# Filter samples on the tensor engine: four channels under one weight load

## The chip, the cores and the metric

One core of a Trainium2 chip runs the whole program. Its engines work side by side and are tied together by semaphores only: TensorE (PE; its weight loads are listed apart as PEld), VectorE (DVE), ScalarE (ACT), GpSimd (POOL) and SyncE (SP), the last two mostly as queues that issue DMAs. The metric is the device time of one execution in microseconds, as the median of several runs.

## The reference, cut to what matters

```python
def _A_ref(u, A_re, A_im, B_re, B_im, C_re, C_im, log_dt, Dskip):      # u: 1 x 2048 x 512
    dt = jnp.exp(log_dt)[:, None]
    A = A_re + 1j * A_im                                               # 512 channels x 128 states
    ...
    P = jnp.exp(logdA[:, :, None] * l[None, None, :])                  # l = 0 .. 2047
    K = jnp.einsum("dn,dnl,dn->dl", Cc, P, dB).real                    # 512 filters of 2048 samples
    ...                                                                # FFT of 4096: y = K * u along l
    y = (lambda x, *d: x.transpose(*d))(y, 0, 2, 1) + u * Dskip[None, None, :]

h = x + _A_ref(_layernorm(x), ...)
return h + _B_ref(_layernorm(h), ...)                                  # _B_ref: layernorm, w1 512x1376, gelu, w2
```

A layer norm, one long filter per channel, a residual, two more norms and an MLP with a residual. The filter K of a channel is the real part of a sum over 128 states of c_n times exp(a_n l). The change is in how samples of K are made.

## The kernel before

The 2048 rows are dealt over 128 partitions, 16 rows each. The filtering runs in the frequency domain with matmuls as transforms: the normed input goes through a first transform (`aps`, written to `A_dram` and read back as `X`), a second (`xps`, matrix `M`), is multiplied by the filter's spectrum (`kfps`), transformed back (`zps`), written to `Zd` and read back as `ZT`, and enters the MLP. The channels are worked in two halves of 256 (`hh` = 0 and 1).

The spectrum isn't computed from all 2048 samples but from some of them. A sample position is split in two: l = 8k + offset with k = 0..31 (tile `Pt`) and twenty offsets (tile `Q`, list `OFFS`). For state n (the partition) and channel c, `Pt[n, k, 0..1, c]` holds exp(8 k a_n) as two real components and `Q[n, m, 0..1, c]` holds c_n exp(OFFS[m] a_n) in the same way; the sum over n of the product of both is a matmul of a channel with itself: 32 rows (k) by 20 columns (m), and its real part is a combination of the two components.

How the operands come about, for each half (the functions are printed below):

- `exps`: ACT writes the amplitudes exp(8 k Re) into `Pt[:, k, 1, :]` (32 instructions of 256 channels) and those of `Q` (20), which DVE multiplies by `amp`. `Pt` and `Q` are one tile each for both halves, so the second half's exponentials wait until the matmuls of the first have read them (`o_get` on `o_kgen`).
- `p_half`, `q_half`: the phases are made on PE as a matmul with the tables `RP` and `RQ` (`outer`, from `wp`, `wq` and a folded identity), ACT takes the sine (`sines`, tiles `s` and `sq` in the ring of buffers `w`, WB = 6), DVE multiplies sine and amplitude (`mul`). For `Pt` the phases are made for k = 16..31 only; the lower k = 15..0 take the same sines with the other sign. A half has eight such steps for `Pt` (32 channels each) and ten for `Q`.
- `kgen`: four blocks a half. A block has 16 x 2 x 4 matmuls: 16 channels, two components, and four groups of channels that sit side by side in the array, each 32 columns wide (`tile_position`). Each matmul has its own weight load, 32 columns taken at a stride of 512 elements from `Pt`, and 20 columns at the same stride from `Q`. The two components stay apart in PSUM; ACT copies one (`ku`) and DVE adds or subtracts the other (`samples`, with `half_sign`). The first samples go to `KD_near`, the far ones to `KD_far`, each as one DMA, and five DMAs bring them back as `kt`, the weights' partner in the spectrum matmuls (`kfps`).

All this is written as some 620 operations with dependencies (`S.op`), and a list `ORDER` written out by hand says in which order they are issued and, where an operation may run on one of two engines, on which: `step >> 2` is the number of the operation, `step & 3` the choice. Every engine executes its share in the order of the list. The costs that stand with the operations are not used at run time. Ahead of `kgen` in the list stand the norms of the input (`norm`, `aps` and its eviction `a`), the parameters (`params`: phases `psi`, amplitude `amp`, the transposes `lps`), the transform tables (`tables`: `M`, `Mn`, `R`, `Rn`; the last rows through `last_row` and `put_rows`), all on the same engines. Behind it come `x_stage`, `conv` and `head_rows`, then `mlp`, which is plain code.

Of the kernel before, what the change touches and what calls it, by code (L numbers as in the profile page):

```python
# [23 lines left out]
TINY = 1e-30  # L24
EPS = 1e-5
# [3 lines left out]
WB = 6  # L29
AT = {"root": 2, "m0": 3, "m1": 3, "bases": 3, "sin0": 3, "exp": (1, 4), "sin": (3, 5)}  # L30
ORDER = [
# [154 lines left out]
def prefix(nc0, S, K, cp, ct, c2):  # L186
# [7 lines left out]
    K.deal = c2.tile([P, 2, 2, 4, 8], bf16, name="deal")  # L194
    g.memset(K.deal[:], 0.0)
    g.affine_select(out=K.deal[:], in_=K.deal[:], pattern=[[-64, 2], [-8, 2], [-16, 4], [-1, 8]], compare_op=ALU.not_equal, fill=1.0, base=0, channel_multiplier=1)
    K.deal = K.deal[:].rearrange("p h s g i -> p (h s g i)")
# [30 lines left out]
    split = ((3, 15), (0, 7), (0, 1), (1, 1), (4, 1))  # L228
    bits = c2.tile([P, 5], i32, name="bits")
    for n, (sh, m) in enumerate(split):  # L230
        ts(nc, bits[:, n:n + 1], pi[:], sh, ALU.logical_shift_right, m, ALU.bitwise_and)
    pf = ct.tile([P, 5], f32, name="pf")
    nc.vector.tensor_copy(pf[:], bits[:])
    t1, q, odd, b1, top16 = (pf[:, n:n + 1] for n in range(5))
    K.half_sign = ct.tile([P, 1], f32, name="half_sign")
    ts(nc, K.half_sign[:], top16, -2.0, ALU.mult, 1.0, ALU.add)
# [33 lines left out]

def outer(nc, S, K, pp, c2):

    K.RP = pp.tile([P, 16, 2, 32], bf16, name="RP")
    K.RQ = pp.tile([P, 20, 2, 16], bf16, name="RQ")
    m = c2.tile([P, 64], bf16, name="m64")
    wp = c2.tile([P, 16, 2], bf16, name="wp")
    wq = c2.tile([P, 20, 2], bf16, name="wq")
    g = nc.gpsimd
    count(nc, wp[0:96], 4, [[8, 16], [0, 2]])
    for n, v in enumerate((63.75, 64.0)):  # L280
        g.memset(wp[96:128, :, n:n + 1], v)
        g.memset(wq[96:128, :, n:n + 1], v)
    g.memset(wq[64:112], 1.0)
    for p0, p1, pieces in ((32, 64, ((0, 0, [[0, 8]]), (8, 1, [[0, 4]]), (12, 2, [[1, 2], [0, 2]]), (16, 4, [[1, 4]]))),
                           (64, 80, ((0, 0, [[0, 8]]), (8, 1, [[0, 4]]), (12, 2, [[1, 2], [0, 2]]), (16, 4, [[1, 4]]))),
                           (0, 48, ((0, 1, [[1, 8]]), (8, 2, [[2, 4]]), (12, 4, [[0, 2], [4, 2]]), (16, 8, [[0, 4]])))):
        for at, base, pattern in pieces:
            cnt = 1
            for _, c in pattern:
                cnt *= c  # L290
            count(nc, wq[p0:p1, at:at + cnt], base, pattern + [[0, 2]])
    pl = S.at(10.2)

    def fold():
        tt(nc, m[:], K.ident[:, 0:64], K.ident[:, 64:128], ALU.add)
        tt(nc, m[:, 0:32], m[:, 0:32], m[:, 32:64], ALU.add)
        tt(nc, m[:, 32:48], m[:, 0:16], m[:, 16:32], ALU.add)

    def make_p():
        tt(nc, K.RP[:].rearrange("p i c d -> p (i c) d"), bc(wp[:].rearrange("p i c -> p (i c)").unsqueeze(2), [P, 32, 32]), bc(m[:, 0:32].unsqueeze(1), [P, 32, 32]), ALU.mult)  # L300
# [38 lines left out]
def tables(nc, S, K, cp, mp, cv, ct, c2, psp, dram):  # L339
# [64 lines left out]
    bf = ct.tile([P, 4, 2, 16], f32, name="bf")  # L404
# [14 lines left out]
    def last_row():  # L419
# [4 lines left out]
        nc.vector.tensor_copy(bs[:], bf[:])  # L424
# [3 lines left out]
    b = S.op("DVE", 1.5, last_row, [f])  # L428
# [39 lines left out]
def params(nc, S, K, cp, pp, sc, cv, psp, raws, ldt, dtb, grb):  # L468
    T, S2, Z = {}, S.op, {}

    def step():
        for h in range(2):
            d = slice(HW * h, HW * h + HW)
            nc.scalar.activation(dtb[:, d].rearrange("p (s g i) -> p g s i", s=2, g=4), ldt[:, d].rearrange("p (g s i) -> p g s i", s=2, g=4), ACT.Exp)

    o_dt = S2("ACT", 0.8, step, [S.at(4.2)], fun=0, bias=600)
    for pair, t0 in ((("are", "aim"), 4.5), (("cre", "cim"), 5.6), (("bre", "bim"), 6.6)):
        cell = {}
        for n, nm in enumerate(pair):
            def tr(cell=cell, nm=nm, n=n):  # L480
                if not n:
                    cell["p"] = psp.tile([P, 2, 512], f32, name=f"tps_{nm}", tag="p", bufs=PB)
                for k in range(4):
                    nc.tensor.matmul(cell["p"][:, n, k::4], lhsT=raws[nm][:, k, :], rhs=K.deal, start=True, stop=True)
# [9 lines left out]
    nc.gpsimd.memset(src_p[:, :, 3, :], 3.0)  # L494
    nc.gpsimd.memset(src_q[:, :, 7, :], 3.0)
# [12 lines left out]
    w = [sc.tile([P, 512], f32, name=f"w{n}", tag="w", bufs=WB) for n in range(6)]  # L508
    t, cre, cim = [x[:] for x in w[0:4]], w[4][:], w[5][:]
    pc = sc.tile([P, 512], f32, name="pc", tag="ko", bufs=2)  # L510
    S.group, last = "six", S.group
    K.o_six = [S.op("NONE", 0.0, lambda: None, acq="w") for _ in range(6)]
# [17 lines left out]
    o_pc = S2(D, 1.5, lambda: frac(pc[:], psi[:], 124.0), [o_psw], bias=B - 20)  # L530
# [84 lines left out]
    def top():  # L615
        for h in range(2):
            d = slice(HW * h, HW * h + HW)
            nc.scalar.copy(K.top[0:1, d].rearrange("p (g s i) -> p g s i", s=2, g=4), cell["k"][:, d].rearrange("p (s g i) -> p g s i", s=2, g=4))
# [802 lines left out]
```

## Time and profile before

| | us |
|---|---|
| median of 3 runs | 273.11 |
| lowest, highest | 272.82, 273.22 |
| the profiled execution | 272.82 |
| its span, first to last instruction | 271.0 |

The profile is of one execution. Its span is 1.8 us shorter than the time of that same run, which also counts what lies around the instructions. PE is busy 236.1 us of the span, DVE 204.9, ACT 173.1, POOL 35.6. A row of a list in order of time begins with the start and the length of a run of like instructions, then engine, line, operation, tile written <- tiles read, shape, count, and in square brackets how long the engine had been idle and what it had waited for; "issue" is time in which it waited for nothing that the profile shows. Lines are those of the kernel printed above; a helper's line (L76, L88, L139) stands for many uses, which the tile names tell apart. The granted clock is that of PE, 1.00 being full speed.

### The profile page before, as it was taken

How to read it: one execution, taken by the hardware profiler on the slowest of the kernel's cores; microseconds unless marked ns; L12 is line 12 of the kernel's file. 1: busy time of each engine (PE TensorE's matmuls, PEld its weight loads, DVE VectorE, ACT ScalarE, POOL GpSimd, SP SyncE). 2: the span in 40 equal slices, each digit the busy share in tenths (PEclk: the TensorE clock that was granted, in tenths of full speed). 3: DMA queues.
4: the chain of work that ended last, by engine and by line, in shares of the span. 5: the costliest groups of instructions: out<-in, count | busy, mean ns of one | idle time of the engine just before them, and what ended most of it. 6: DMA issues, size and time to landing. Idle time of an engine off the chain costs nothing.

```text
span 271.0 us, 6046 instructions
## 1 busy us (share of the span) xinstructions
PE 236.1 (87%) x2380; PEld 151.6 (56%) x2380; DVE 204.9 (76%) x426; ACT 173.1 (64%) x293; POOL 35.6 (13%) x96
## 2 busy tenths in 40 slices
PE   3898348768769977999999999978999999999995
PEld 3433012325558754779988888766954444444443
DVE  4899999999999999998195969968572772772022
ACT  2999999998958999992644473716822621631710
POOL 8803850000001100000551001000000000000000
PEclk9755555999956999999999999999999999999999
DMA  5804945676957300120178598769824014014101
GB/s 160 284 3 60 182 131 155 175 217 213 290 182 212 64 0 0 41 80 5 51 175 228 182 232 236 193 177 285 213 41 114 2 40 116 0 22 102 34 19 59
DMA packets 50568, 33.71 MB, mean 124 GB/s; under 512 B 22602, under 2 KB 49084, under 8 KB 50284
## 3 DMA queue, kind: packets, MB, share of 16 engines
q1 hardware_dynamic: 49036, 29.69, 40.5%
q0 software_dynamic: 1504, 3.64, 5.2%
q8 instruction: 18, 0.29, 0.5%
q14 instruction: 10, 0.08, 0.1%
HBM read 18.65 MB, written 11.26 MB: 110 GB/s over the span
## 4 chain that ended last, share of the span: by engine, by line
PE 47%; DVE 30%; DMA 8%; issue 7%; ACT 5%; SPq 2%; DVEq 0%; ACTq 0%
PE h1ps L1228 14%; PE o2ps L1241 13%; PE kps L752 6%; DVE X L88 4%; DMA Zd<-z 4%; DVE st L819 4%; PE kfps L921 3%; DVE w L76 2%; DVE Q L670 2%; DVE a L88 2%; DVE Pt L76 1%; ACT sq L139 1%; ACT s L139 1%; DVE u L832 1%; DMA ZT<-Zd 1%
## 5 line engine op out<-in xcount | busy, mean ns | idle before, releaser
L1231 ACT ACTIVATE hT<-h1ps,b_sb 128x512 bf16<-128x512 f32 (+3 forms) x55 | 31.9, 604 | 40.8 <-PE h1ps L1228 40.8
L1228 PE MATMUL h1ps<-y2T,wide 128*128 128x512 bf16 (+3 forms) x220 | 40.7, 336 | 0.6 <-ACT y2T L86 0.5
L921 PE MATMUL kfps<-kt,M 128*128 128x256 bf16 x320 | 39.1, 273 | 0.0
L1241 PE MATMUL o2ps<-w_sb,hT 128*128 128x512 bf16 (+3 forms) x187 | 38.7, 366 | 0.0
L921 PEld LDWEIGHTS <-M 128*128 128x128 bf16 x320 | 31.3, 98 | 6.1 <-issue 2.6
L76 DVE TENSOR_TENSOR ot<-o2ps,h 128x512 bf16<-128x512 f32 (+1 forms) x17 | 10.9, 657 | 30.0 <-PE o2ps L1241 17.7
L1228 PEld LDWEIGHTS <-wide 128*128 128x128 bf16 (+1 forms) x220 | 21.9, 100 | 17.2 <-issue 0.6
L1241 PEld LDWEIGHTS <-hT 128*128 128x128 bf16 (+1 forms) x187 | 18.3, 98 | 19.7
L658 ACT ACTIVATE Pt<-th 128x256 bf16<-128x256 f32 x64 | 20.7, 401 | 2.6 <-DVE th L76 2.5
L752 PE MATMUL kps<-Q,Pt 128*32 128x20 bf16 x1024 | 19.1, 221 | 3.5 <-issue 2.6
L837 PE MATMUL aps<-u,BD 128*128 128x512 bf16 x32 | 12.1, 468 | 10.9 <-ACT u L830 6.9
L752 PEld LDWEIGHTS <-Pt 128*32 128x32 bf16 x1024 | 18.4, 169 | 5.6 <-issue 4.9
L139 ACT ACTIVATE sq<-qv 128x1024 bf16<-128x1024 int16 x20 | 20.3, 1069 | 0.2 <-PE qv L723 0.2
L76 DVE TENSOR_TENSOR Pt<-s,Pt 128x1024 bf16<-128x1024 bf16 x32 | 20.2, 683 | 0.0
L86 ACT CAST z<-zps 128x1024 bf16<-128x1024 f32 (+1 forms) x13 | 12.1, 957 | 8.3 <-PE zps L951 5.9
L139 ACT ACTIVATE s<-pv 128x1024 bf16<-128x1024 int16 x16 | 16.1, 1056 | 0.3 <-DVE Q L76 0.3
L76 DVE TENSOR_TENSOR h<-y,X 128x512 f32<-128x512 f32 (+1 forms) x12 | 9.3, 774 | 8.1 <-PE y L1192 6.0
L86 ACT CAST kf<-kfps 128x1024 bf16<-128x1024 f32 (+1 forms) x8 | 7.7, 959 | 10.4 <-PE kfps L921 10.3
L837 PEld LDWEIGHTS <-BD 128*128 128x128 bf16 x32 | 2.8, 103 | 19.1 <-DVE BD L76 6.6
L689 PE MATMUL pv<-RP,PQ 128*128 128x512 bf16 x32 | 10.8, 437 | 3.0 <-ACT sq L139 0.7
L76 DVE TENSOR_TENSOR Q<-sq,Q 128x1024 bf16<-128x1024 bf16 x20 | 13.3, 681 | 0.0
L442 POOL DMA_DIRECT2D Dp<-Dd x24 | 11.9, 503 | 9.1 <-DMA Dd<-ds 8.0
(234 smaller groups left out, 466.3 us busy)
## 6 DMA issues: line engine op xcount, KB each, us to landing
A_dram<-a SPq DMA_DIRECT2D x16, 256.0 KB, 2.5
X<-A_dram SPq DMA_DIRECT2D x4, 1024.0 KB
Zd<-z SPq DMA_DIRECT2D x15, 256.0 KB, 3.6
ZT<-Zd SPq DMA_DIRECT2D x11, 256.0 KB, 4.0
x<-in_A_u_dram SPq DMA_DIRECT2D x4, 512.0 KB, 7.8
X<-in_A_u_dram SPq DMA_DIRECT2D x4, 512.0 KB, 4.6
out_dram<-ot SPq DMA_DIRECT2D x15, 128.0 KB, 1.7
ZT<-Zd POOLq DMA_DIRECT2D x5, 256.0 KB, 5.0
```

Source lines behind the costliest of these rows:

```text
L76: (nc.vector if e == "DVE" else nc.gpsimd).tensor_tensor(out, a, b, op)
L86: nc.scalar.copy(out, in_)
L88: nc.vector.tensor_copy(out, in_)
L139: nc.scalar.activation(out, v.bitcast(i16)[..., 0:2 * n:2], ACT.Sin, scale=S2PI / 65536)
L442: nc.gpsimd.dma_start(t[o::128 // cnt], bass.AP(row.tensor, row.offset + 1024 * kh, [[0, cnt], [1, 1024]]))
L658: nc.scalar.activation(K.Pt[:, k, 1, :], K.th[:, ds], ACT.Exp, scale=float(8 * k))
L752: nc.tensor.matmul(kps[32 * g:32 * g + 32, i // 8, at:at + 20], lhsT=Pt[:, :, u, c], rhs=Q[:, :, u, c], start=True, stop=True, tile_positi ...
L837: nc.tensor.matmul(ps[:, h, :], lhsT=K.BD[:, h].rearrange("p a b -> p (a b)"), rhs=cell["u"][:], start=True, stop=True)
L921: nc.tensor.matmul(ps[:, k, c, :], lhsT=K.M[:, t, k0 + k, c, :], rhs=kt[:, t, :], start=(c == 1 and t == 0), stop=(t == 4))
L1228: nc.tensor.matmul(pt[:fs, 0:n], lhsT=K.w1_sb[:, dc, fc * P:fc * P + fs], rhs=(y2T[tb][:, dc, js, :] if tb or js.start else K.y2T[:, dc]). ...
L1231: nc.scalar.activation(hT[tb % 2][:fs, fc, cols], pt[:fs, 0:n], ACT.Gelu_apprx_tanh, bias=K.b1_sb[:fs, fc:fc + 1], scale=1.0)
L1241: nc.tensor.matmul(pt[:], lhsT=h[:fs, fc, jj * P:(jj + 1) * P], rhs=K.w2_sb[:fs, fc, d], start=(fc == 0), stop=(fc == NFC - 1))
```

## The change

Four channels are now the columns of one weight load: `Pt` is laid out as component, group of four channels, k, channel, so that 32 k times 4 channels lie in one piece of 128. One matmul multiplies it with the 20 offsets of the same four channels, 80 columns. Of the 128 x 80 results the blocks where both channels are the same are used. Component 0 and 1 go into the same PSUM columns one after the other, so their sum is formed there; for that sum to be the real part the phases are turned by an eighth of a turn (`EIGHTH`, `TURN`).

```diff
+TURN = 9.0
+EIGHTH = (21.125, 21.375)
-WB = 6
+WB = 4
...
-        K.Pt = big.tile([P, 32, 2, HW], bf16, name="Pt", tag="b1")
+        K.Pt = big.tile([P, 2, HW // 4, 32, 4], bf16, name="Pt", tag="b1")
...
-                nc.scalar.activation(K.Pt[:, k, 1, :], K.th[:, ds], ACT.Exp, scale=float(8 * k))
+                nc.scalar.activation(K.Pt[:, 1, :, k, :], K.th[:, ds].rearrange("p (e g) -> p e g", g=4), ACT.Exp, scale=float(8 * k))
...
-                hi = K.Pt[:, 16:32, :, dq]
-                tt(nc, hi, s[:], bc(hi[:, :, 1:2, :], [P, 16, 2, 32]), ALU.mult)
-                lo = K.Pt[:, 15::-1, :, dq]
-                tt(nc, lo, s[:], bc(lo[:, :, 1:2, :], [P, 16, 2, 32]), ALU.mult)
+                cell["s"] = sc.tile([P, 2, 8, 16, 4], bf16, name="s", tag="w", bufs=WB)
...
+                s, e = cell["s"], slice(8 * b, 8 * b + 8)
+                hi = K.Pt[:, :, e, 16:32, :].rearrange("p u e k g -> p u e (k g)")
+                tt(nc, hi, s[:].rearrange("p u e i g -> p u e (i g)"), bc(hi[:, 1:2], [P, 2, 8, 64]), ALU.mult)
+                for u in range(2):
+                    tt(nc, K.Pt[:, u, e, 15::-1, :], s[:, 1 - u], K.Pt[:, 1, e, 15::-1, :], ALU.mult)
...
-        for hv in range(2):
-            def mms(s=s, hv=hv):
...
-                for i in range(16):
+        for b in range(4):
+            e0 = 32 * s + 8 * b
+            def mms(s=s, b=b, e0=e0):
+                kps = cell[s, b] = psp.tile([P, 8, 128], f32, name="kps", tag="p", bufs=PB)
+                for e in range(8):
                     for u in range(2):
-                        at = 64 * (i % 8) + 32 * u
-                        for g in range(4):
-                            c = 128 * s + 32 * g + 16 * hv + i
-                            nc.tensor.matmul(kps[32 * g:32 * g + 32, i // 8, at:at + 20], lhsT=Pt[:, :, u, c], rhs=Q[:, :, u, c], start=True, stop=True, tile_position=(0, 32 * g))
-            def real(s=s, hv=hv):
-                cell["u"] = sc.tile([P, 20, 16], f32, name="ku", tag="w", bufs=WB)
-                nc.scalar.copy(cell["u"][:], ...)
-            def out(s=s, hv=hv):
...
-                stt(nc, cell["all"][:, :, d], v, K.half_sign[:], cell["u"][:], ALU.mult, ALU.add)
-            m = S.op("PE", 2.6, mms, K.o_p[s] + K.o_q[s], acq="p")
+                        nc.tensor.matmul(kps[:, e, 0:80].rearrange("p (g m) -> p g m", g=4), lhsT=K.Pt[:, u, e0 + e].rearrange("p k g -> p (k g)"),
+                                         rhs=K.Q[:, :, u, 4 * (e0 + e):4 * (e0 + e) + 4].rearrange("p m g -> p g m"), start=(u == 0), stop=(u == 1))
+            def out(e, s=s, b=b, e0=e0):
...
+                evac(nc, e, cell["all"][:].rearrange("p g m j -> p (g m) j")[:, :, e0:e0 + 8], cell[s, b][:, :, 0:80].rearrange("p e x -> p x e"))
+            m = S.op("PE", 0.7, mms, [K.o_p[s][b], K.o_q[s][b], K.o_q[s][4]], acq="p")
...
-            q(e).dma_start(far[:]...)
-            q(e).dma_start(near[:], cell["all"][:, 0:8])
+    def put(e, g):
+        q(e).dma_start(KD[hh][32 * g:32 * g + 32].rearrange("p (r c) -> p r c", r=4)[:, :, 0:320], cell["all"][g::4, g].rearrange("p (r s) j -> p r (s j)", s=5))
...
-        K.o_kt[hh].append(S.op(either, (0.46, 0.8), lambda e, t=t: get(e, t), [w[0 if t < 2 else 1]] + K.o_kt[hh][:1], lat=2.5, acq="kt" if t == 0 else None))
+        K.o_kt[hh].append(S.op(either, (0.46, 0.8), lambda e, t=t: get(e, t), w + K.o_kt[hh][:1], lat=2.5, acq="kt" if t == 0 else None))
...
-    part("xload", x_load, A_dram, change, [K.o_bd, K.o_bt] + K.o_ph)
+    part("xload", x_load, A_dram, change, [K.o_bd, K.o_bt, K.o_last] + K.o_ph)
```

Along with it: the channel order in `dtb`, `top` and `deal` follows the new layout; the tables `wp`, `wq`, `RP` (now two instructions) and `OFFS` are reordered; six working tiles of `params` move to one tile `five` and two in the ring `w`, which shrinks from six buffers to four; two small tiles are shared with others, for which the load of `X` now also waits for `last_row`.

A block is now 16 matmuls (eight groups of four channels, two components) and waits only for its own products of `Pt` and `Q` and the common fifth one of `Q`; there are eight blocks a half. One eviction of 128 x 640 takes the place of `ku` and `samples`. Four puts, one for each channel of a group, take the place of two, and every get waits for all four.

`ORDER` is written anew, 634 steps. Counted out against the operations, what the rest of the text speaks of is this:

| | before | after |
|---|---|---|
| evictions of `kps` | 8 on ACT and 8 on DVE (`ku`, `samples`) | 14 on ACT, 2 on DVE |
| evictions of `aps` (16) | 6 on DVE | 2 on DVE |
| norms of x (`u`, 16) | 12 on DVE | 15 on DVE |
| first eviction of `lps`, that of `dps` | DVE | ACT |
| `Mn`; the second half of `M` 1 (L374) | ACT, ACT | DVE, DVE |
| on DVE ahead of the last product of half 0: table products (`M<-base,Dp`), `last_row`, `Mn` | none of them | two of six, both others |
| evictions of `xps` between the first exponential and the last sine of half 1, on ACT | 0 | 2 |
| evictions of `kps` in the same stretch, on ACT | 1 (`ku`) | 3 |
| half 0: puts and gets of the samples | put and get 1 on POOL, the others on SP | puts 2, 0, 3 and gets 2, 1 on POOL; put 1, gets 0, 3, 4 on SP |
| SP, half 0 | X loads 1 to 3, last rows out, X load 4, put, gets, `put_rows` | last rows out, X loads 1 to 3, put, get 0, X load 4, `put_rows`, gets 3, 4 |
| half 1: puts and gets | all but one get on SP | all but one get on SP |
| PE behind the last phase matmuls of half 1 | a block, a spectrum, a block, two x stages, a block | a spectrum, two blocks, an x stage, a block, an x stage, a block |
| idle matmul pairs ahead of the MLP | 9 | 5 |

Some evictions of `xps`, `kfps` and `zps` change between ACT and DVE in either direction.

More of the change, by code (lines that the diff above doesn't have):

```diff
@@ L227, in prefix @@
         at += n
-    split = ((3, 15), (0, 7), (0, 1), (1, 1), (4, 1))
-    bits = c2.tile([P, 5], i32, name="bits")
+    split = ((3, 15), (0, 7), (0, 1), (1, 1))
+    bits = c2.tile([P, 4], i32, name="bits")
     for n, (sh, m) in enumerate(split):
         ts(nc, bits[:, n:n + 1], pi[:], sh, ALU.logical_shift_right, m, ALU.bitwise_and)
-    pf = ct.tile([P, 5], f32, name="pf")
+    pf = ct.tile([P, 4], f32, name="pf")
     nc.vector.tensor_copy(pf[:], bits[:])
-    t1, q, odd, b1, top16 = (pf[:, n:n + 1] for n in range(5))
-    K.half_sign = ct.tile([P, 1], f32, name="half_sign")
-    ts(nc, K.half_sign[:], top16, -2.0, ALU.mult, 1.0, ALU.add)
+    t1, q, odd, b1 = (pf[:, n:n + 1] for n in range(4))
     cols = ct.tile([P, 5], f32, name="cols")
@@ L507, in params @@
     psi0, q0 = (cv.tile([P, 512], f32, name=nm, tag="pa", bufs=2) for nm in ("psi0", "q0"))
[L508 to L510 removed]
+    five = sc.tile([P, 5, 512], f32, name="five", tag="ko", bufs=1)
+    t, pc = [five[:, n] for n in range(4)], five[:, 4]
+    cre, cim = [sc.tile([P, 512], f32, name=f"w{n}", tag="w", bufs=WB)[:] for n in range(2)]
     S.group, last = "six", S.group
[L512 removed]
+    K.o_six = [S.op("NONE", 0.0, lambda: None, acq="w" if n > 3 else None) for n in range(6)]
     S.group = last
@@ L638, in params @@
     K.o_src = K.o_ql + K.o_pl + K.o_raw
-OFFS = list(range(1, 9)) + [258, 260, 262, 264, 516, 520, 772, 776, 1032, 1288, 1544, 1800]
+OFFS = [x for r in range(4) for x in (1 + 2 * r, 258 + 2 * r, (516, 520, 772, 776)[r], 2 + 2 * r, 1032 + 256 * r)]
 def exps(nc, S, K, big, hh, gate):
@@ L766, in kgen @@
             mm.append(m)
-            r = S.op("ACT", 0.45, real, [m] + ends, acq="w")
-            ends.append(S.op("DVE", 0.5, out, [r], rel=[m, r], acq="ko" if not s and not hv else None))
+            ends.append(S.op(("ACT", "DVE"), (0.75, 0.75), out, [m] + (K.o_raw if first else ends[:1]), rel=[m], acq="ko" if first else None))
     K.o_kgen = mm
     ds = slice(HW * hh, HW * hh + HW)
-    far, near = KD[hh]
     def q(e):
         return nc.sync if e == "SP" else nc.gpsimd
-    def put(e, n):
-        if n:
-            q(e).dma_start(far[:].rearrange("t p r c -> p t (r c)"), cell["all"][:, 8:20].rearrange("p (t r) c -> p t (r c)", t=3))
-        else:
-            q(e).dma_start(near[:], cell["all"][:, 0:8])
+    def put(e, g):
+        q(e).dma_start(KD[hh][32 * g:32 * g + 32].rearrange("p (r c) -> p r c", r=4)[:, :, 0:320], cell["all"][g::4, g].rearrange("p (r s) j -> p r (s j)", s=5))
@@ L785, in get @@
             K.kt[hh] = cv.tile([P, 5, HW], bf16, name="kt", tag="kt", bufs=2)
-        src = near[:].rearrange("(g k) r c -> (k r) g c", g=4)[128 * t:128 * t + 128] if t < 2 else far[t - 2].rearrange("(g k) r c -> (k r) g c", g=4)
+        if t < 2:
+            src = KD[hh][:].rearrange("(g k) (r c) -> (k r) g c", g=4, r=8)[128 * t:128 * t + 128, :, 0:64]
+        else:
+            at = (64, 128, 256)[t - 2]
+            src = KD[hh][:].rearrange("(g k) (r c) -> (k r) g c", g=4, r=4)[:, :, at:at + 64]
         q(e).dma_start(K.kt[hh][:, t, :].rearrange("p (g c) -> p g c", g=4), src)
     either = ("SP", "POOL")
-    w = [S.op(either, (0.46, 0.8), lambda e, n=n: put(e, n), ends, rel=[ends[0]], lat=2.5) for n in range(2)]
+    w = [S.op(either, (0.46, 0.8), lambda e, g=g: put(e, g), ends, rel=[ends[0]], lat=2.5) for g in range(4)]
     K.o_put = w
@@ L802, in norm_in @@
     sm = lp.tile([P, 16, 2], f32, name="sm")
-    df = lp.tile([P, 16], f32, name="df")
+    df = ve
     def roots():
@@ L1294 @@
     K.Dd = dram.tile([P, 2, 128], bf16, name="Ds")
-    KD = [(dram.tile([3, P, 4, 64], bf16, name=f"KD_far{h}"), dram.tile([P, 8, 64], bf16, name=f"KD_near{h}")) for h in range(2)]
+    KD = [dram.tile([P, 1536], bf16, name=f"KD{h}") for h in range(2)]
     Zd = [dram.tile([32, P, HW], bf16, name=f"Zd{h}") for h in range(2)]
```

82 lines of the change are left out of this document (37 added, 45 removed), and 44 rows, old and new, of the table ORDER.

## The prediction

> **What bounds the kernel now.** I read the page first, then the windows by stage, then the instructions in order of time around the filter samples.
>
> ```profile
> span 271.0 us, 6046 instructions
> ...
> PE 236.1 (87%) x2380; PEld 151.6 (56%) x2380; DVE 204.9 (76%) x426; ACT 173.1 (64%) x293; POOL 35.6 (13%) x96
> ...
> q8 instruction: 18, 0.29, 0.5%
> ```
>
> The 87% of PE is no answer: it averages stages with different limits. The windows show them (stretch, its length, then busy time of PE, weight loads, DVE, ACT and POOL, the granted clock, DMA share, GB/s):
>
> ```profile
> 40.00:60.00 20.00, 15.03 (x65) 5.56 (x65) 20.00 (x35) 19.94 (x25) 0.00 (x0) 0.79 0.61 171
> ...
> 65.00:84.00 19.00, 14.42 (x536) 11.81 (x536) 18.91 (x35) 13.12 (x15) 0.00 (x0) 0.78 0.73 219
> 84.00:100.00 16.00, 14.28 (x108) 10.81 (x107) 15.70 (x17) 15.99 (x53) 1.56 (x2) 0.94 0.33 88
> 100.00:110.00 10.00, 8.03 (x60) 5.19 (x60) 9.93 (x18) 9.97 (x12) 0.00 (x0) 1.00 0.01 2
> 110.00:133.00 23.00, 22.68 (x619) 18.83 (x616) 18.15 (x33) 16.69 (x21) 1.22 (x1) 1.00 0.14 37
> ...
> 163.00:177.00 14.00, 13.07 (x118) 11.16 (x115) 12.96 (x28) 7.21 (x9) 0.98 (x2) 1.00 0.79 210
> 177.00:271.00 94.00, 88.93 (x508) 49.24 (x508) 47.63 (x127) 35.70 (x63) 0.48 (x1) 1.00 0.33 88
> ```
>
> Ahead of 65 us DVE and ACT are both full (the first row). From 84 to 110 they are full again: ACT makes the exponentials of the second half, which may start only when the matmuls of the first half have read Pt and Q. From 110 PE is full until the MLP, whose 94 us the change leaves alone. Between 65 and 84 ACT is idle for 6 us. That hole is what can be won:
>
> ```profile
> 70.45 2.32 PE L752 MATMUL kps<-Q,Pt 128*32 128x20 bf16 x128 [0.32 <-ACT sq L139]
> ...
> 75.02 0.79 PE L752 MATMUL kps<-Q,Pt 128*32 128x20 bf16 x36
> 77.02 2.32 PE L752 MATMUL kps<-Q,Pt 128*32 128x20 bf16 x128 [1.21 <-issue]
> 80.75 1.72 PE L752 MATMUL kps<-Q,Pt 128*32 128x20 bf16 x92 [1.41 <-issue]
> ```
>
> ```profile
> 73.11 0.67 DVE L76 TENSOR_TENSOR Q<-sq,Q 128x1024 bf16<-128x1024 bf16 x1
> 73.71 0.68 DVE L70 TENSOR_SCALAR Rn<-R 128x2048 bf16<-128x2048 bf16 x1
> 74.44 0.55 DVE L118 SCALAR_TENSOR_TENSOR samples<-kps,half_sign,ku 128x320 bf16<-128x320 f32 x1
> 74.91 3.70 DVE L76 TENSOR_TENSOR M<-base,Dp 128x1024 bf16<-128x1024 bf16 x6
> 78.53 1.28 DVE L422 TENSOR_REDUCE bf<-nn 128x32 f32<-128x64 f32 x4
> ```
>
> ```profile
> 71.19 1.09 ACT L139 ACTIVATE sq<-qv 128x1024 bf16<-128x1024 int16 x1
> ...
> 82.97 1.28 ACT L126 ACT_TABLE_LOAD   x1
> 84.26 1.95 ACT L658 ACTIVATE Pt<-th 128x256 bf16<-128x256 f32 x6
> ```
>
> The last product of the half ends on DVE at 73.78, the first exponential starts at 84.26: 10.5 us, with the last two blocks of 2.32 us on PE, the end of the block and the x stage ahead of them (to 75.02), and two waits of 1.21 and 1.41 us for "issue". Those I read as PE running out of instructions: 0.29 MB over 4,760 PE instructions is 61 bytes each, one of the 18 packets of that queue (16 KB) holds some 260, and one block is 256, fetched while the DMA share is 0.73.
>
> **The change part by part.** What counts is from one start to the next: on DVE the duration less 0.08.
>
> *The matmuls.* 1024 pairs of a 32-column load and a 20-column matmul become 256 pairs of 128 and 80. The old pair and a full-size one:
>
> ```profile
> 70.40:72.80 2.40, 2.32 (x128) 2.22 (x127) 1.00 1.04 346
> 77.00:79.40 2.40, 2.32 (x128) 2.22 (x128) 0.50 0.46 145
> ...
> 64.18 0.61 PE L723 MATMUL qv<-RQ,PQ 128*128 128x128 bf16 x8
> ```
>
> A block takes 2.32 us at clock 1.00 and at 0.50; less 0.22 for the last one's own duration that is 16.5 ns a pair, 66 ns for the four that make up the 80 columns of a new pair. The third row has full loads with 128 contiguous columns: (0.61 - 0.22)/7 = 56 ns. So a new pair costs at least 35 ns (56 x 80/128) and at most 66, if its columns, as far apart in Q as before, are read no slower than now. I take 56, the row with the new weight load: 16 pairs are 0.9 us a block, 128 are 7.2 a half against 8.5; ends 4.5 and 8.5. The Trainium skill (Advanced Engine Details and Errata, SBUF Cachelines) says that elements which each lie on another 16-byte line are read at a penalty. The row at both clocks agrees with it, and by that rule the time would be that of the second rival.
>
> *Instructions.* 1,536 fewer for PE, six packets; a half's filter matmuls are one packet, not four. The two waits leave the path; I keep 0.5 us for one that remains.
>
> *Products and exponentials.* The lower product of 1024 elements becomes two of 512, in runs of four, backwards in k, and the exponentials write such runs.
>
> ```profile
> 171.68 0.42 DVE L76 TENSOR_TENSOR pa<-X,kf 128x512 bf16<-128x512 bf16 x1 [0.34 <-ACT kf L86]
> ...
> 10.66 0.69 DVE L76 TENSOR_TENSOR w<-w,w 128x512 f32<-128x512 f32 x1
> ...
> L474 ACT ACTIVATE M<-M x2: 399/408/417, 3.9 to 4.2; 128x256 bf16<-128x256 bf16 x2
> L658 ACT ACTIVATE Pt<-th x64: 398/400/418, 7.2 to 99.9; 128x256 bf16<-128x256 f32 x64
> ```
>
> A product of 1024 is 0.60; two of 512 are 2 x 0.34 at the bf16 row's rate and 2 x 0.61 at one element a cycle (the fp32 row). The runs stay even and contiguous, so I take the first: +0.08 x 8 a half; the other end is +0.62 x 8 = 5.0. Exponentials written in runs of eight (the third row) take 0.408, written in one piece 0.400: I take no change for runs of four; the other end doubles the 0.21 of their 256 elements.
>
> *Eviction.* ku on ACT and samples on DVE (0.55), eight each, go; sixteen of 640 elements come, fourteen on ACT. By a straight line between the first two rows one takes 0.72:
>
> ```profile
> L756 ACT COPY ku<-kps x8: 425/442/545, 67.9 to 132.2; 128x320 f32<-128x320 f32 x8
> ...
> L86 ACT CAST a<-aps 128x1024 bf16<-128x1024 f32 x10 | 9.8, 1045 | 0.0
> ...
> L830 ACT ACTIVATE u<-x,mv,rs 128x512 bf16<-128x512 bf16 x4 | 3.2, 830 | 0.0
> ...
> 57.74 1.21 DVE L88 CAST a<-aps 128x1024 bf16<-128x1024 f32 x1
> 58.87 0.40 DVE L832 TENSOR_SCALAR u<-x,mv,rs 128x512 bf16<-128x512 bf16 x1
> ```
>
> *The new order, first half.* DVE ahead of the last product: four evictions of aps leave (-4 x 1.13), one of lps (-0.6, like 1024 elements at the bf16 rate), one of dps (-0.2), one samples (-0.47); three norms come (+3 x 0.32), two table steps of two products (+2.4), Mn (+0.6, as Rn), the last-row sums (+1.4), the split (+0.6). Sum +0.2: 74.0. ACT ahead of the last sine (end 72.28): +4 x 0.98 - 3 x 0.80, +1.0 and +0.35 for lps and dps, -0.44 for a ku, less 1.0 in which it waited for kps: +1.4, 73.7; with the two products behind it the last one ends at 74.6. Six blocks may follow from the third product from the end on, 72.7. Seven evictions on ACT, 0.6 apart, would end at 77.9 if PE kept up; PE lets the seventh end at 72.7 + 5 x 0.9 + 0.2 + 0.72 = 78.1. Table load 1.28, instruction wait 0.5: exponentials from 79.9 instead of 84.26. **-4.4.**
>
> *Second half.* Before its last sine ACT gets two evictions of xps (+1.9) and three of kps (+1.8) for one ku (-0.4); others change places: +3.3. PE's tail after the last phase matmuls (now 119.3 to 131.6):
>
> ```profile
> 94.21 1.25 PE L921 MATMUL kfps<-kt,M 128*128 128x256 bf16 x10
> ...
> 119.32 1.03 PE L689 MATMUL pv<-RP,PQ 128*128 128x512 bf16 x4
> 120.28 2.51 PE L752 MATMUL kps<-Q,Pt 128*32 128x20 bf16 x128
> ...
> 129.33 2.32 PE L752 MATMUL kps<-Q,Pt 128*32 128x20 bf16 x128
> ```
>
> Three old blocks (7.0), a spectrum (2.4: 22 matmuls at 0.11) and two x stages (1.75), 11.1 in all, become four new blocks (3.6), the same spectrum and x, 7.7. **-3.4 + 3.3 = -0.1.** Behind it PE has the same matmuls as before, on a full engine until 177: 0. Four fewer idle matmul pairs ahead of the MLP, whose output nothing reads: 0.
>
> *Queues.* Every get now awaits four puts. In the first half three puts and two gets stand on POOL; on SP the last load of X stands behind a get, then put_rows, which waits for the last table step, and behind it two gets.
>
> ```profile
> 133.22 2.88 DMA KD_near<-samples
> ...
> 84.90 0.79 POOL L779 DMA_DIRECT2D KD_far<-samples  x1 [47.51 <-DVE samples L118]
> ```
>
> Three issues of 0.8 and a landing of 2.9 from 78.9 on: puts land near 84.3, that load is issued near 85, and the filter is there near 91.5, ahead of the first spectrum (94). It lies under DVE's list up to the second half's first product: four table steps 4.8, eleven evictions of 1.13, one of 0.8, two scalings 1.2, five Q products 3.0 and a spectrum's four 1.9 make 24.1, to 98.7. Cost nothing; without that cover up to 4. Second half: eviction 0.7, four puts 1.6, landing 2.9, gets 2, landing 2.9 are some 10 us, under four spectra, three back stages and an x stage of PE (4 x 2.4 + 4 x 0.87 = 13.1): nothing, with 3 to spare.
>
> Sum: 272.82 (the profiled run: span 271.0 and 1.8 around it) - 4.5 = **268.3**; the median of the runs, 273.11, is 0.3 higher, within their spread.
>
> **Rivals.** *Deeper:* pairs at 35 ns, no instruction wait, so the evictions on ACT end the first half (79.2, -5.1); the tail is 6.4 (-4.7), and of ACT's extra 3.3 only 1.0 counts, the rest in its idle time of 110 to 133: 264.0. For it: that hole. Against: ACT is full from 84 to 110.
>
> *It doesn't share what it says:* PE pays 66 ns a pair and only the order and the fetches gain: exponentials at 80.8 (-3.5), a tail of 8.4 (-2.7 + 3.3): 269.9. For it: the equal time at both clocks. Against: loads of 32 columns may set that time.
>
> *Products at one element a cycle:* DVE's last product is 4.3 later, exponentials at 84.2, and DVE's list of the second half (8 x 1.28, 10 x 0.60, two spectra 4, two evictions 1.9: 22.2) grows by 5.0 and ends at 98.7 + 4.3 + 27.2 = 130.2, the last block at 131.3: no change, 272.5. Against: 16-bit data, unit steps, as in the row of 0.42.
>
> *Slower:* exponentials in runs of four take 0.61: 32 a half on an ACT that ends last in both, +6.7 each: 281.7. It decides from +0.07, 0.47 each. For it: no ACT write of 8-byte runs is among the rows. Against: 32-byte runs cost 0.008.
>
> **How the numbers follow.** Forecast 0.34, deeper 0.22, not sharing 0.22, products 0.07, exponentials 0.07, and 0.08 for four sine buffers in place of six making ACT wait: 0.3 us for each of a half's 18 sines is 5.4 a half, of which the hole in the first half covers none, so 273.5 to 275. A measurement tells 0.2%, 0.55 us, from no change. Faster is the first three, 0.78; same 0.05; slower 0.17. The range, 263.0 to 274.0, holds the first four and half of the last; some 0.07 lies below and 0.11 above.
>
> **What would show it.** Kps as 256 matmuls, 35 to 66 ns from start to start; the second half's first exponential near 80; no "issue" above 1 us inside kps; half products at 0.42, exponentials at 0.40; the MLP from 172.5 instead of 177, its 94 us unchanged. Wrong if half products take 0.69, exponentials above 0.47, ACT waits for products between 50 and 74, or PE idles for kt behind the last kps block.

## The result, and the profile after

The changed kernel takes 293.37 us (median of 4 runs, 293.34 to 293.84) where the kernel before takes 272.97 beside it: a ratio of 1.076, 95% interval 1.073 to 1.079. It is 7.6% slower. The forecast was 268.3, and the range ended at 274.0.

First the page of the changed kernel, then the filter samples' tile with its operations (duration in ns as minimum, median and maximum, then first and last start).

```profile
span 291.5 us, 4492 instructions
...
PE 256.5 (88%) x1604; PEld 164.9 (57%) x1604; DVE 203.8 (70%) x436; ACT 178.0 (61%) x298; POOL 35.7 (12%) x96
...
q8 instruction: 12, 0.20, 0.3%
```

```profile
L748 PE MATMUL kps<-Q,Pt x256: 295/315/325, 67.1 to 150.7; 128*128 128x80 bf16 x128
...
L88 ACT CAST samples<-kps x14: 692/692/727, 73.6 to 151.0; 128x640 bf16<-128x640 f32 x14
```

The instructions went as the diff says: 256 matmuls for 1024, 12 instruction packets for 18, 640-element evictions of 0.69 us. The time is in the matmuls themselves. PE's instructions in order of time, around the end of the first half and near the end of the second:

```profile
67.08 2.35 PE L748 MATMUL kps<-Q,Pt 128*128 128x80 bf16 x16 [0.32 <-ACT s L141]
...
72.87 15.54 PE L748 MATMUL kps<-Q,Pt 128*128 128x80 bf16 x112 [0.33 <-ACT s L141]
...
147.09 0.42 PE L866 MATMUL xps<-X,Mn 128*128 128x256 bf16 x1
147.30 0.42 PE L867 MATMUL xps<-X,M 128*128 128x256 bf16 x1
...
148.58 2.39 PE L748 MATMUL kps<-Q,Pt 128*128 128x80 bf16 x16
```

Seven blocks of 16 pairs take 15.54 us without a gap: (15.54 - 0.315)/111 = 137 ns from one pair to the next, where 56 was forecast and 66 was the upper end. The first block, alone at 67.08 while the granted clock was 1.00, has the same: (2.35 - 0.315)/15 = 136. The clock stands third from the end in these rows of line 748 alone:

```profile
67.00:69.30 2.30, 2.22 (x16) 1.70 (x15) 1.00 0.51 171
...
79.40:81.60 2.20, 2.20 (x18) 1.99 (x17) 0.50 0.14 40
```

The eviction rows on ACT show who waits:

```profile
84.05 0.69 ACT L88 CAST samples<-kps 128x640 bf16<-128x640 f32 x1 [1.50 <-PE kps L748]
86.25 0.69 ACT L88 CAST samples<-kps 128x640 bf16<-128x640 f32 x1 [1.51 <-PE kps L748]
86.96 1.28 ACT L128 ACT_TABLE_LOAD   x1
88.44 2.56 ACT L657 ACTIVATE Pt<-th 128x256 bf16<-128x256 f32 x8 [0.20 <-PE kps L748]
```

ACT stands still for 1.5 of every 2.2 us, and the second half's first exponential starts at 88.44 (79.9 forecast, 84.26 before). The windows by stage (stretch, length, busy time of PE, weight loads, DVE, ACT and POOL, granted clock, DMA share, GB/s):

```profile
67.00:88.40 21.40, 19.94 (x137) 16.49 (x137) 11.28 (x21) 11.72 (x15) 0.00 (x0) 0.66 0.53 167
...
132.00:151.00 19.00, 18.86 (x129) 14.86 (x127) 9.88 (x19) 8.19 (x9) 0.00 (x0) 0.77 0.05 15
...
198.00:291.00 93.00, 88.83 (x509) 49.12 (x507) 49.40 (x133) 35.95 (x64) 0.48 (x1) 1.00 0.34 89
```

PE is nearly full in both stretches of filter samples (93% and 99%) while DVE and ACT are about half idle. The MLP is as it was and starts at 198 instead of 177. Of these 21 us, 4.2 have arisen when the exponentials start, and 15 more between there and the end of the last filter block (150.97 by the last row above, 131.65 before). Of the 15, 128 x (137 - 66) ns, 9.1 us, are pairs. Another part is the clock: the x-stage rows at 147 start 0.21 us apart, at a granted clock near a half, where the same matmuls before started 0.11 apart. The two x stages there, 16 matmuls, cost 1.6 us by that. The other 4 us or so are not placed by these rows. The spectra's matmuls and evictions alone (busy time of PE, DVE and ACT with the counts, then clock, DMA share, GB/s) show the lower clock too:

```profile
144.00:156.00 12.00, 5.21 (x26) 0.00 (x0) 0.30 (x1) 0.51 0.12 34
156.00:198.00 42.00, 27.65 (x240) 6.08 (x5) 6.96 (x8) 1.00 0.71 190
```

200 ns each against 115, so 26 of them cost 2.2 us; they lie behind the last filter block.

### The profile page after: what moved, and what is told of

Same layout as the page of the kernel before. It is cut to its first block, busy times and chain, and to the rows that moved or that the text cites. A ratio compares the mean times of both kernels' runs of the same rounds, so it can differ in the third digit from the quotient of the medians.

```text
span 291.5 us, 4492 instructions
## 1 busy us (share of the span) xinstructions
PE 256.5 (88%) x1604; PEld 164.9 (57%) x1604; DVE 203.8 (70%) x436; ACT 178.0 (61%) x298; POOL 35.7 (12%) x96
## 4 chain that ended last, share of the span: by engine, by line
PE 58%; DVE 22%; ACT 8%; DMA 6%; issue 3%; SPq 2%; DVEq 0%; ACTq 0%
PE h1ps L1218 13%; PE o2ps L1231 12%; PE kps L748 12%; PE kfps L911 7%; DVE X L90 4%; DVE st L809 3%; DMA Zd<-z 3%; ACT s L141 3%; DVE five L78 2%; ACT sq L141 2%; ACT a L88 2%; DVE M L78 1%; PE aps L827 1%; DMA M<-in_A_C_im_dram 1%; PE pv L687 1%
## 5 line engine op out<-in xcount | busy, mean ns | idle before, releaser
L911 PE MATMUL kfps<-kt,M 128*128 128x256 bf16 x320 | 41.5, 282 | 0.0
L748 PE MATMUL kps<-Q,Pt 128*128 128x80 bf16 x256 | 36.3, 314 | 1.0 <-ACT s L141 0.6
L911 PEld LDWEIGHTS <-M 128*128 128x128 bf16 x320 | 32.4, 101 | 5.8 <-issue 1.0
L748 PEld LDWEIGHTS <-Pt 128*128 128x128 bf16 x256 | 30.8, 120 | 6.5 <-issue 1.5
L78 DVE TENSOR_TENSOR Pt<-s,Pt 128x512 bf16<-128x512 bf16 (+1 forms) x48 | 22.9, 508 | 3.5 <-ACT s L141 2.9
L88 ACT CAST samples<-kps 128x640 bf16<-128x640 f32 x14 | 9.7, 694 | 19.1 <-PE kps L748 19.1
L88 ACT CAST a<-aps 128x1024 bf16<-128x1024 f32 x14 | 14.5, 1044 | 0.2 <-PE aps L827 0.2
L721 PE MATMUL qv<-RQ,PQ 128*128 128x512 bf16 (+1 forms) x64 | 11.5, 298 | 3.6 <-ACT sq L141 2.0
```

The source lines that it names most:

```text
L78: (nc.vector if e == "DVE" else nc.gpsimd).tensor_tensor(out, a, b, op)
L88: nc.scalar.copy(out, in_)
L721: nc.tensor.matmul(v[:, n], lhsT=K.PQ[hh][:, b + n, :], rhs=K.RQ[:, m0:m1].rearrange("p i c d -> p (i c d)"), start=True, stop=True)
L748: nc.tensor.matmul(kps[:, e, 0:80].rearrange("p (g m) -> p g m", g=4), lhsT=K.Pt[:, u, e0 + e].rearrange("p k g -> p (k g)"), rhs=K.Q[:, : ...
L911: nc.tensor.matmul(ps[:, k, c, :], lhsT=K.M[:, t, k0 + k, c, :], rhs=kt[:, t, :], start=(c == 1 and t == 0), stop=(t == 4))
```

## The experiments

The theories. **A**: in the moving operand (`Q`, whose columns stream past the loaded weights), a column that lies 1 KB from the one before costs 137/80 = 1.7 ns, whatever the PE clock. **B**: a full load with an accumulating matmul costs a fixed 137 ns. **C**: the load of 128 columns isn't overlapped. A second question is why the old 66 ns for four pairs was no upper bound. Readings **D** and **E**, quoted with the runs below, answer that.

**Four channels innermost.** The changed kernel walks 20 responses m inside each channel; this one walks the four channels, which are neighbours in Q, inside each m. The result is the same.

```diff
-matmul(kps[:, e, 0:80].rearrange("p (g m) -> p g m", g=4), ...
-       rhs=K.Q[:, :, u, 4*(e0+e):4*(e0+e)+4].rearrange("p m g -> p g m"), ...)
+matmul(kps[:, e, 0:80].rearrange("p (m g) -> p m g", g=4), ...
+       rhs=K.Q[:, :, u, 4*(e0+e):4*(e0+e)+4], ...)
-evac(all as "p (g m) j" [:, :, e0:e0+8], kps[:, :, 0:80] as "p x e")
+evac(all[:, :, :, e0:e0+8], kps[:, :, 0:80] as "p e (m g) -> p g m e")
```

> The same 80 columns per pair, but read in the order m outside and channel inside, so that four neighbouring columns lie in 8 consecutive bytes of Q; PSUM takes them in that order and the eviction sorts them. Theory A (each column of the moving operand that lies 1 KB from the one before costs 137/80 = 1.7 ns): only 20 such jumps are left, a pair falls to 35 to 66 ns, the evictions of kps set the end of the first half, its last one starts near 78 instead of 86.25, the clock is not lowered from 74 on, and the time is 264 to 272 us. Theory B (a full load followed by an accumulating matmul costs a fixed 137 ns): pair 137 ns, time 293 us. Theory C (the load of 128 columns, 0.12 us, is not overlapped): the same, 137 ns and 293 us.

It takes 263.14 us (6 runs, 263.03 to 264.06), 0.9615 of the kernel before, run again beside it (0.956 to 0.967): faster than both kernels. PE's rows of the first half, then ACT's:

```profile
66.85 0.74 PE L748 MATMUL kps<-Q,Pt 128*128 128x80 bf16 x16 [0.32 <-ACT s L141]
...
72.57 3.71 PE L748 MATMUL kps<-Q,Pt 128*128 128x80 bf16 x96 [0.18 <-ACT sq L141]
```

```profile
72.39 4.30 ACT L88 CAST samples<-kps 128x640 bf16<-128x640 f32 x7
76.71 1.28 ACT L128 ACT_TABLE_LOAD   x1
78.00 2.56 ACT L657 ACTIVATE Pt<-th 128x256 bf16<-128x256 f32 x8
```

A pair takes (0.74 - 0.20)/15 = 36 ns, with the same full load and the same accumulation. That ends B and C. The sorting costs the evictions next to nothing (median 0.72 us in place of 0.69). Seven evictions now run on ACT without a wait, and the exponentials start at 78.0.

**No jumps at all.** 80 neighbouring channels of one row of Q; PSUM, eviction, loads and accumulation are the changed kernel's.

```diff
-rhs=K.Q[:, :, u, 4*(e0+e):4*(e0+e)+4].rearrange("p m g -> p g m")
+rhs=K.Q[:, 16 + e % 4, u, 128*s + 8*b:128*s + 8*b + 80]
```

> The moving operand is 80 neighbouring channels of one row m of Q (another result; loads, evictions, DMAs and waits stay). Theory A: the floor of the pair without any jump, about 56 ns as in the full-size matmuls of 128 columns at the full clock, 35 at the least; time 264 to 270 us. Theories B and C: 137 ns, 293 us.

264.47 us (one run). The matmuls start 35 to 36 ns apart within each of the 16 blocks, so runs of four leave nothing to gain in the pair. The 56 ns that the expectation still took for the floor belong to 128 columns, 0.44 ns each; 80 of them are 35 ns, so the full load adds nothing that shows.

**Half the columns in one component.**

```diff
+mh = 20 - 10 * u
-rhs=K.Q[:, :, u, ...]
+rhs=K.Q[:, 0:mh, u, ...]
```

> The second component's matmul takes only the first 40 of the 80 columns, at the same distance of 1 KB (the other 40 hold the first component alone). Theory A, a price per column: starts alternate 137 and 69 ns, a block of 16 takes 1.65 us instead of 2.2, time about 286 us. Theories B and C, a price per pair: 137 ns throughout and 293 us.

282.64 us (one run), some 3 us less than the 286 expected; the pairs are as A has them. Starts alternate between 137 and 70 to 72 ns, and the seven blocks that took 15.54 us take 11.81:

```profile
72.07 11.81 PE L749 MATMUL kps<-Q,Pt 128*128 128x80 bf16 x112 [0.33 <-ACT s L141]
```

A price per column, 1.7 ns: 40 of them are 69 ns, so at most 3 ns a pair are fixed.

**A narrow load.**

```diff
+nk = 32 - 24 * u
-matmul(kps[:, e, ...], lhsT=K.Pt[:, u, e0+e] ..., start=(u == 0), stop=(u == 1))
+matmul(kps[0:4*nk, e, ...], lhsT=K.Pt[:, u, e0+e, 0:nk] ..., start=True, stop=True)
```

> The second component's load has 32 columns of weights in place of 128, its matmul writes 32 partitions, and each matmul overwrites instead of adding (the result holds the first component alone in 96 partitions and the second alone in 32). Theory A: 137 ns for all pairs, time 293 us. Theory B (accumulation): all pairs fall alike. Theory C (the load): the pairs with the narrow load fall to some 40 to 70 ns, the others stay at 137.

319.14 us (one run), and about 229 ns for every pair (224 to 232), which no theory had. The edit changes three things at once: loads of 128 and of 32 columns take turns, half of the matmuls write 32 partitions, and each overwrites what the one before has just written. Which of them costs the extra 92 ns stays open. The run tells nothing of B and C; the runs of four do.

**What were the old 66 ns?** Three kernels on the base of the kernel before: flat columns, flat loads (flat: taken from neighbouring places), and one column tile at a time (a column tile is one of the four groups of 32 array columns).

```diff
 # flat columns
-rhs=Q[:, :, u, c]
+rhs=Q[:, 16 + i % 4, u, 128*s + 32*g:128*s + 32*g + 20]
 # flat loads
-lhsT=Pt[:, :, u, c]
+lhsT=Pt[:, i, u, 128*s + 32*g:128*s + 32*g + 32]
 # one column tile at a time
-for i in range(16): for u in range(2): for g in range(4):
+for g in range(4): for i in range(16): for u in range(2):
```

> The kernel before, with each matmul's 20 columns taken as 20 neighbouring channels of one row m of Q (another result; loads, number of matmuls and their places in PSUM as before). Reading D (the 66 ns for four matmuls in four column tiles were the far-apart columns, read by the four at the same time: 4 x 20 x 1.7 = 137 one after another, about half of that because they overlap): four matmuls fall from 66 to some 36 ns, a block of 128 from 2.32 to about 1.4 us, time some 3 us less than before. Reading E (the 66 ns were four loads of 32 columns, or issue, and the columns hid below them): 66 ns stay, time as before, 272 to 274 us.

> The kernel before, with each load's 32 columns of weights taken as 32 neighbouring channels of one row of Pt instead of 32 columns 1 KB apart (another result; the matmuls read Q as before). Reading D: 66 ns for four, as before. Reading E with loads that pay for their own far-apart columns: the four fall to 40 ns or less. If neither this nor the flat columns alone changes the 66 ns, it is the issue of eight instructions.

> The kernel before with the loop over the four column tiles moved outside the other two, so that 32 matmuls in a row use one column tile; same matmuls, same result. Reading D: nothing overlaps any more, 20 columns cost 20 x 1.7 = 34 ns or more, a block of 128 takes 4.4 us or more instead of 2.32, and the time grows by 10 us or more. Reading E: a block stays near 2.32 us and the time near 273.

The second block of each (128 pairs), in that order; the block before was 2.32 us:

```profile
69.94 1.99 PE L752 MATMUL kps<-Q,Pt 128*32 128x20 bf16 x128
```

```profile
70.24 1.35 PE L752 MATMUL kps<-Q,Pt 128*32 128x20 bf16 x128
```

```profile
76.20 8.00 PE L752 MATMUL kps<-Q,Pt 128*32 128x20 bf16 x128
```

Less a last duration of 0.20, over 32 groups of four: 56, 36 and 244 ns (270.63, 269.73 and 324.16 us, one run each, with 272.91 for the kernel before beside them). With flat loads the four matmuls' 4 x 20 jumping columns cost at most 36 ns, about 20 x 1.7 and not 80 x 1.7: the four column tiles read at the same time. With flat matmuls the far-apart loads are left: 56 ns for the four, as much as 32 x 1.75, so they overlap too. With one tile at a time a pair takes 61 ns by itself, near the price of its own load. So D was right that four streams overlap, and E was right that loads set most of the 66; D's 36 ns for flat columns and E's unchanged 66 both missed.

**Both flat** (the first two edits together).

> The kernel before with both the 32 columns of the load and the 20 of the matmul taken from neighbouring places (another result). If far-apart columns of load and matmul set the 66 ns for four between them (36 ns were left with flat loads, 57 with flat matmuls): the four fall below 36 ns, to 20 to 30, and the waits for instructions in the third and fourth block, which grew from 1.4 to 2.8 us as the pairs got shorter, stay or grow; time 268 to 271 us.

```profile
74.80 0.42 PE L752 MATMUL kps<-Q,Pt 128*32 128x20 bf16 x36
78.42 1.23 PE L752 MATMUL kps<-Q,Pt 128*32 128x20 bf16 x128 [3.20 <-issue]
81.87 0.91 PE L752 MATMUL kps<-Q,Pt 128*32 128x20 bf16 x92 [2.22 <-issue]
```

274.0 us (one run, with a median of 274.74 for the kernel before beside it), above the 268 to 271 expected. Four pairs take 32 ns, half of before, so the 36 ns with flat loads were hardly more than what is left with nothing far apart. And yet these two blocks last from 74.80 to 82.78, where before they ran from 75.02 to 82.47. The waits grew by more than the work shrank: 1.21 and 1.41 us before, 3.20 and 2.22 here. The trace says what they end with. In both kernels each of the two waits ends 1.4 to 1.6 us after a 16 KB packet of the instruction queue has landed (at 75.58 and 79.19 us before, at 76.88 and 80.42 here), and so they do in the runs with flat columns and with flat loads. So in the kernel before, it was the arrival of instructions that set the end of the third and fourth block, not the pair.

**Two channels at a time.**

```diff
-rhs=K.Q[:, :, u, ...].rearrange("p m g -> p g m")
+rhs=K.Q[:, :, u, ...].rearrange("p m (x y) -> p x m y", x=2)
```

> As the kernel with runs of four, but two neighbouring channels at a time: 40 jumps of 1 KB and 40 neighbours in a pair; each eviction is split in two of 320 elements. If every jump costs 1.7 ns: 40 x 1.7 = 69 ns or more a pair. If two columns in 4 bytes are enough to hide the jump: 36 ns as with runs of four. The time matters less here, since the split evictions add some 0.4 us each.

```profile
71.37 8.07 PE L748 MATMUL kps<-Q,Pt 128*128 128x80 bf16 x112 [0.33 <-ACT s L141]
```

(8.07 - 0.25)/111 = 70 ns, 270.6 us (one run): 40 jumps at 1.75 ns. The second column of a run is free, and it doesn't hide the jump. One estimate fits all of these runs: a pair takes the longer of 0.44 ns a column and 1.75 ns a jump. With runs of four the 20 jumps make 35 ns, just what the 80 columns need anyway. The Trainium skill (Advanced Engine Details and Errata, SBUF Cachelines) says that at least two hits on a 16-byte line are needed to absorb the latency. Here two did not absorb it: 70 ns a pair with runs of two, 36 with runs of four.

**Sixteen bytes apart.** Every eighth channel, so that each column lies on the line next to the last one's.

```diff
-rhs=K.Q[:, :, u, 4*(e0+e):4*(e0+e)+4].rearrange("p m g -> p g m")
+rhs=K.Q[:, 16:20, :, 128*s + 4*e + u:128*s + 4*e + u + 73:8]
```

> The changed kernel with the 80 columns taken 16 bytes apart (every eighth channel, in runs of ten, from four rows m and both components; another result; loads, PSUM, evictions as in the changed kernel). If any column that lies outside the 16 bytes of the one before costs 1.7 ns, however near: 137 ns a pair and about 293 us. If the price comes from the distance of 1 KB: 36 to 60 ns and 263 to 268 us.

```profile
73.10 16.37 PE L748 MATMUL kps<-Q,Pt 128*128 128x80 bf16 x112 [0.20 <-ACT s L141]
```

295.98 us (one run): (16.37 - 0.32)/111 = 145 ns a pair. So the distance of 1 KB isn't what costs; a step of 16 bytes already costs as much. Where between 2 and 16 bytes the price sets in, no run shows.

**The same reads, scattered in PSUM.** Only the walk of the matmul is turned; PSUM and the eviction keep the changed kernel's order.

```diff
-matmul(kps[:, e, 0:80].rearrange("p (g m) -> p g m", g=4), ... rhs=K.Q[...].rearrange("p m g -> p g m"))
+matmul(kps[:, e, 0:80].rearrange("p (g m) -> p m g", g=4), ... rhs=K.Q[...])
```

> As the kernel with runs of four, but PSUM keeps the order of the changed kernel (channel outside, m inside): neighbouring columns are written 80 bytes apart, and the eviction is untouched, so that only the order in which the matmul walks is changed. If only the reads of Q cost: 36 ns a pair and 263 us. If a write to PSUM that jumps with every column costs as much as a read that jumps: 137 ns and 293 us; in between, a price of its own.

```profile
71.37 7.91 PE L748 MATMUL kps<-Q,Pt 128*128 128x80 bf16 x112 [0.33 <-ACT s L141]
```

(7.91 - 0.27)/111 = 69 ns, 268.63 us (one run). Each column is now written 80 bytes on from the last, or 236 bytes back after every fourth; that costs 0.86 ns a column. Against the kernel before, measured beside each, this edit of the matmul alone wins 6.1 us where the runs of four win 10.9: for the rest the eviction, not the matmul, has to do the sorting.

**Evictions shared with DVE** in the kernel with runs of four: three entries of the order give their evictions to DVE.

```diff
-    1212, 1220, 1236 in ORDER
+    1213, 1221, 1237
```

> The kernel with runs of four, and three of the seven evictions of kps that ACT takes at the end of the first half given to DVE, at their places in the order. Theory F (with 36 ns a pair the evictions on ACT set the end of the first half, as the prediction's deeper rival had it): the first exponential moves from 78.0 to about 76.3, the end of the last pair, and the time falls by up to 1.7 us, to 261.4 to 262.5. Rival G (DVE's list behind them, 2.2 us longer, ends last in the second half): the exponentials start earlier but the last product of the second half does not, time 263 to 265.

0.9701 of the kernel before (0.965 to 0.976), 266.08 us: no better than the runs of four (0.956 to 0.967), and above what F and G allowed. ACT, PE and DVE, and last the row of DVE with the seven evictions on ACT:

```profile
76.89 2.56 ACT L657 ACTIVATE Pt<-th 128x256 bf16<-128x256 f32 x8 [1.00 <-PE kps L748]
...
86.96 1.01 ACT L88 CAST X<-xps 128x1024 bf16<-128x1024 f32 x1 [2.00 <-issue]
...
96.86 1.28 ACT L141 ACT_TABLE_LOAD   x1
```

```profile
85.84 0.27 PE L865 MATMUL xps<-X,M 128*128 128x256 bf16 x1 [0.70 <-DVE X L90]
```

```profile
75.25 1.54 DVE L90 CAST samples<-kps 128x640 bf16<-128x640 f32 x2
...
77.91 0.81 DVE L90 CAST samples<-kps 128x640 bf16<-128x640 f32 x1
...
84.58 2.34 DVE L90 CAST X<-xps 128x1024 bf16<-128x1024 f32 x2
```

```profile
82.69 2.35 DVE L90 CAST X<-xps 128x1024 bf16<-128x1024 f32 x2
```

The exponentials do start 1.1 us earlier, so F was right on the first half. But then ACT waits 2.00 us, and the table load behind stands at 96.86 (95.87 with the seven evictions on ACT). The profile names nothing for that wait; the order of the list does. ACT's next step is to evict the x stage whose eight matmuls PE starts at 85.84 (83.96 with the seven on ACT), and it starts when they are done. PE itself had waited for DVE to free the buffer by an eviction of `X`. That one stands 1.9 us later (84.58 for 82.69), since DVE, which is busy without a gap from 78 to 95, has three evictions of 0.8 us more ahead of it. So it is G's cause, DVE's longer list, that takes the gain, and it does so already within the exponentials. It also ends last in the second half, as G said: DVE's products of `Pt` there last until 1.8 us later (the last starts at 123.4 for 121.6), and so do the last filter matmuls (124.9 for 123.1). The rest of the profiled run's 3.5 us lies in the MLP, where some matmuls ran at a lower granted clock (`h1ps` up to 417 ns for 381).

## Why the prediction was wrong, step by step

**The step that failed** is the bound of the pair: "at least 35 ns (56 x 80/128) and at most 66, if its columns, as far apart in Q as before, are read no slower than now". The 66 ns were taken for the reading of 80 columns. They were 32-column loads and 20-column matmuls, each with four of them at once: at most 36 ns for the reads by themselves, 56 for the loads. Put into one stream the same 80 columns take 80 x 1.7 = 137. The change gave up the four parallel readers along with the four instructions. The row stood in the prediction: a block takes the same 2.32 us at clock 1.00 and 0.50, so PE's clock set neither term, and 66/80 could have been four streams as well as one. The 56 ns came from a row with contiguous columns, which these are not.

**The penalty for far-apart columns**, of which the Trainium skill speaks (Advanced Engine Details and Errata, SBUF Cachelines), was weighed and then priced wrongly. I let the old 66 ns stand for it, hence 269.9. The runs agree that there is a penalty and put it at 1.7 ns a column, 137 a pair. The same holds of PSUM: the Trainium skill (PSUM — Partial Sum Buffer, Specifications, the row on cachelines) says that a non-contiguous pattern slows matmuls significantly; 69 against 36 ns agrees.

**What held.** With the pair at 36 ns, the kernel lands at 263.1, where the deeper rival (35 ns, evictions on ACT ending the first half, no instruction wait) said 264.0, with the exponentials at 78.0 for its 79.2. So the rest of that sum stands to about 1 us, in part by luck: the exponentials came 1.2 us earlier than it had them, and what lies behind gained some 0.4 us less. The single terms, in the changed kernel:

```profile
L657 ACT ACTIVATE Pt<-th x64: 398/402/421, 5.9 to 107.3; 128x256 bf16<-128x256 f32 x64
L78 DVE TENSOR_TENSOR Pt<-s,Pt x48: 405/424/691, 44.4 to 141.1; 128x512 bf16<-128x512 bf16 x32, 128x1024 bf16<-128x1024 bf16 x16
...
  issue: 1.5, 3
```

```profile
40.00:60.00 20.00, 14.92 (x64) 5.62 (x65) 19.43 (x41) 19.99 (x24) 0.00 (x0) 1.00 0.75 187
60.00:67.00 7.00, 4.52 (x22) 1.75 (x22) 6.93 (x18) 6.83 (x10) 0.00 (x0) 1.00 0.70 198
```

```profile
74.25 0.68 DVE L78 TENSOR_TENSOR Q<-sq,Q 128x1024 bf16<-128x1024 bf16 x1
```

Half products take 0.42 and exponentials in runs of four 0.40, so the rivals of products and exponentials fall. ACT is busy for 26.8 of the 27 us to 67, so four sine buffers make it wait for nothing. The last product of the first half ends at 74.93 (74.6 forecast), and an eviction is 0.69 (0.72). The instruction waits go: PE's matmuls of the filter samples wait for nothing but sines and each other, and the three waits for "issue" above, 1.5 us together, stand with the weight loads. The two of 2.6 us that I let go were what ended the first half of the kernel before, as the run with both flat showed.

**The filter's way through memory** cost nothing, as forecast. All that the spectra's matmuls and their weight loads waited for in the changed kernel is two waits for "issue", 1.0 us together, and none for `kt`:

```profile
L911 PE MATMUL kfps<-kt,M x320: 270/273/421, 104.4 to 193.9; 128*128 128x256 bf16 x160
its engine sat idle before it (us, times) until:
  issue: 1.0, 2
```

**Not foreseen at all**: the lower clock around the slow pairs. The changed kernel's spectra reach 421 ns; with runs of four no one takes over 273:

```profile
L911 PE MATMUL kfps<-kt,M x320: 270/273/273, 91.7 to 163.8; 128*128 128x256 bf16 x160
```

On this base the clock stayed at 1.00 around the filter samples with pairs of 36 and 70 ns and fell to 0.50 there for long stretches with pairs of 104 ns on average and more. But slow pairs aren't the only thing that goes with it. The kernel before was granted 0.50 from 20 to 40 us, ahead of its first filter matmul at 65, and with the 36 ns pairs of the run without jumps matmuls of the MLP reached 417 ns for 381. What lowers the clock stays open.

## What to carry to other kernels

Here a matmul's time per column was set by how its operands lie, 1.7 ns against 0.44, and not by PE's clock: walk the index that is contiguous in SBUF innermost, keep the PSUM side contiguous too, and let the eviction sort. Before moving work from one engine to another, look at what the second one then holds up. Before merging matmuls in column tiles into one, ask what they did at the same time; a block's time divided by its columns is not the price of a column when four streams share it. When a time doesn't follow the clock, find what it follows before using it as a bound.

## What the runs showed of the hardware

- A moving column that lies 16 bytes or 1 KB from the one before costs 1.8 or 1.7 ns, the 1.7 alike at granted clocks of 1.00 and 0.50. Contiguous, or in runs of four bf16, a column costs 0.45 ns; runs of two give 0.88 on average.
- Loads of weights pay too: four loads of 32 columns 1 KB apart, in four column tiles at once, take 56 ns; with neighbouring columns the four pairs take 32. Four column tiles read at the same time, for loads as for matmuls: 66 ns for four pairs, against 244 with 32 in a row in one tile.
- Writes to PSUM that jump 80 bytes forward, or 236 back, with each column cost 0.86 ns a column.
- A full 128-column load adds nothing that shows to a pair of 36 ns, though its own row lasts 96 ns: 80 contiguous columns at 0.44 ns make 35.
- PE can run out of instructions: in the kernel before, two waits of 1.2 and 1.4 us each end some 1.5 us after a 16 KB packet of the instruction queue has landed.
